# Lending one of four PSUM banks to the weight conversion during the first block

## The chip, the cores and the metric

The kernel runs on one core of one Trainium2 chip. The metric is the time of one execution on that core in microseconds (us), as the median of several runs. A core has five engines that run side by side, each through its own instructions in order: TensorE (PE) multiplies matrices into PSUM, VectorE (DVE), ScalarE (ACT) and GpSimd (POOL) work on elements, and SyncE (SP) issues transfers. PSUM has eight banks; a bank holds 512 numbers of 32 bits in each of 128 partitions. SBUF is the large working memory.

## The reference

The first part is causal attention with a forget gate, for 4 batches, 8 heads, 576 positions and 64 numbers per head; then two layers on the 2304 tokens follow, each 512 to 2048 to 512:

```python
scores = scale * np.matmul(q, k.transpose(0, 1, 3, 2))
cum = np.cumsum(np.maximum(s, 0.0), axis=-1)
bias = -(cum[:, :, :, None] - cum[:, :, None, :])
scores = np.where(causal, -1000000000.0, scores + np.minimum(bias, 0.0))
attn = softmax(scores)                   # max, exp, sum, divide
x = np.matmul(attn, v)                   # tokens x 512

h = x @ w_in;  g = s * relu(h)**2 + b;                      x = g @ w_out
h = x @ w_in2; g = relu(h) + alpha * np.minimum(h, 0.0);    out = g @ w_out2
```

The four weight matrices come as 64-bit floats, which the kernel reads as pairs of 32-bit words.

## The kernel before

*Attention* is cut into 32 units (batch, half of the queries, pair of heads). For each head of a unit, `scores` multiplies q and k into a PSUM bank (`sc`), reduces on DVE with the bias (L461), takes exponentials on ACT (L473), and normalises on POOL (L484). `values` transposes the probabilities on PE into a bank (`pt`, L515), copies them to SBUF (L519) and multiplies with v into `av` (L531), from where `xf` is filled (L546).

*The layers* go by blocks of 256 or 512 tokens and by f, 16 slices of 128 of the 2048 columns. `up` multiplies x and w_in (L783), squares the positive part, and splits the result into a high part gh (ACT) and a rest gl (POOL, L131); `down` multiplies with w_out into the accumulators `acc` (L897). Numbers are multiplied in a short 32-bit format, so everything is split into such a pair first. In layer 2 the blocks of 512 tokens take Strassen's seven products: a pair of f has three PSUM tiles, a, b, c (L854); `up_first` multiplies products 1, 6, 5 into a, b, c and `up_second` adds products 7, 2, 3, 4 (L813). The trace names the tiles p and the right-hand sides xs.

*The weights* of layer 1 are converted while the warm-up and block 0 run: 16 packets of a w_in and a w_out slice. `convert` rescales the high words on ACT (L140), then DVE shifts the result left by 3 in place (L141), and DVE takes the low words shifted right by 29 and ors them in (L142). `load_packet` then splits the result: the high part on ACT (L130), the rest on DVE for w_in and on POOL for w_out (L131). Packets 0 to 3 are traced within attention's warm-up (units 0 to 3), packet f + 4 behind `up(f)` of block 0.

*PSUM:* two banks for `acc`, one for `hp`, one for `av`, and four buffers of the tag `b`, for score tiles, transposes, column sums, the wide block's `hp` and layer 2's tiles.

*The order of work* is not as written: a planner with its own model of time goes through all instructions at build time and writes out a fixed order for each engine, in which the trace's order of the source is a priority. A tile of a tag with several buffers gets one that the planner sees free when the tile is first written; a tile of a tag with one buffer waits until the last user of that buffer is done. Each engine then takes its instructions in that order and waits on semaphores. Attention is drawn along by the loop over n = block * 16 + f (L987), which advances it until a share of the units has been traced (`pace`).

Of the kernel before, what the change touches and what calls it, by code (L numbers as in the profile page):

```python
# [19 lines left out]
def tile_forget_attention__then__two_mlps(  # L20
# [79 lines left out]

    def load_constants():
        nc.sync.dma_start(out=gate_s, in_=act_s.partition_broadcast(P))
        nc.sync.dma_start(out=gate_b, in_=act_b.partition_broadcast(P))
        nc.sync.dma_start(out=nalpha, in_=alpha.rearrange("(f p) -> p f", p=P))
        nc.vector.tensor_scalar(out=nalpha, in0=nalpha, scalar1=-1.0, scalar2=None, op0=ALU.mult)
        nc.vector.tensor_scalar(out=gate_s, in0=gate_s, scalar1=1.0 / W_SCALE, scalar2=None, op0=ALU.mult)
        nc.vector.tensor_scalar(out=gate_b, in0=gate_b, scalar1=1.0 / W_SCALE, scalar2=None, op0=ALU.mult)

    def sum_gates(first):
# [13 lines left out]
        tp = ps.tile([P, 5, B * H], F32, tag="b", bufs=4, name="tp")  # L123
# [10 lines left out]
    def convert(raw, wt):  # L134

        low, high = raw[:, :, 0], raw[:, :, 1]

        nc.scalar.activation(wt.bitcast(F32), high.bitcast(F32), AF.Prelu, scale=REBASE, alpha=-(2.0**32))  # L140
        nc.vector.tensor_scalar(out=wt, in0=wt, scalar1=3, scalar2=None, op0=ALU.logical_shift_left)  # L141
        nc.vector.scalar_tensor_tensor(  # L142
            out=wt, in0=low, scalar=29, in1=wt, op0=ALU.logical_shift_right, op1=ALU.bitwise_or
        )
# [71 lines left out]
    def load_packet(layer, f):  # L216
# [3 lines left out]
        for n, src in enumerate((wi, wo)):  # L220
# [7 lines left out]
            convert(src, wt)  # L228
# [8 lines left out]
    def sum_columns():  # L237
# [5 lines left out]
        total = ps.tile([P, 512], F32, tag="b", name="colsum", bufs=4)  # L243
# [4 lines left out]
        turned = ps.tile([P, 512], F32, tag="b", name="colsum_t", bufs=4)  # L248
# [29 lines left out]
    class Unit:  # L278
# [21 lines left out]
        def bank(self, tag, name):  # L300
# [9 lines left out]
            return ps.tile([P, 512], F32, tag="b", name=name, bufs=4)  # L310
# [449 lines left out]
    def mlp_block(layer, t, x):  # L760
# [11 lines left out]
        def up(f):  # L772
            w = packet(layer, f)
            if layer == 0 and count == 1:
                hp = ps_h.tile([P, 512], F32, tag="hp", name=f"hp{layer}_{t}_{f}")
            else:
                hp = ps.tile([P, 512], F32, tag="b", name=f"hp{layer}_{t}_{f}", bufs=4)
# [68 lines left out]
        def up_first(f):  # L846
# [7 lines left out]
            a, b, c = (ps.tile([P, 512], F32, tag="b", name=f"p{z}_{name}", bufs=4)[:, :T] for z in range(3))  # L854
# [132 lines left out]
    for n in range(len(BLOCKS) * NF):  # L987
# [4 lines left out]
        late.append((down, finish, f, up(f)))  # L992
        if layer == 0 and t == 0 and f + AHEAD < NF:
            with tc.issue_after(relus[f - 1]) if f else nullcontext():
                packet(0, f + AHEAD)
            for g in range(f + AHEAD + 1, min(f + AHEAD + 3, NF)):
                fetch(0, g)
        if n == NF - 2:
# [53 lines left out]
```

## Time and profile before

| what | us |
|---|---|
| median of three runs | 1041.06 |
| lowest, highest run | 1039.58, 1042.63 |
| the profiled execution | 1040.97 |
| its span, first to last instruction | 1039.2 |
| PE busy in it | 1019.4 |
| DVE busy in it | 681.3 |
| ACT busy in it | 672.4 |
| POOL busy in it | 457.6 |

Up to about 61 us PE works on attention's units 0 to 3 and on filler products (L97). Block 0's first product starts at 61.67 us. The profile gives each engine's busy time; an instruction that stands and waits for a port of the memory counts as busy, so its duration is to be compared with the shortest of its kind. PE's matmuls overlap one another; that PE is busy does not mean that it goes at full rate.

### The profile page before, as it was taken

Reading aid. Unit: us, or ns where it says so; the run is one execution under the profiler, and the core shown is the slowest. Engines: PE = TensorE matmul, PEld = TensorE weight load, DVE = VectorE, ACT = ScalarE, POOL = GpSimd, SP = SyncE. Lnnn points to the kernel's source line nnn. Section 1 sums busy time; section 2 is a strip of 40 time slices with the busy share of each in tenths; the row PEclk is TensorE's granted clock in tenths of the full one; section 3 lists DMA queues with packets and bytes.
Section 4 is the critical chain, followed back from the end, with each engine's and each line's share of the span. In section 5 each row is a group of like instructions: output and inputs, shape, how many; then the busy total and the mean of one; then the engine's idle time right before and its main releaser. Section 6 shows DMA issues by size and latency. Waiting matters only on the chain. (4 is left out here: it accounts for less than half of the span.)

```text
span 1039.2 us, 20636 instructions
## 1 busy us (share of the span) xinstructions
PE 1019.4 (98%) x6952; PEld 925.8 (89%) x6952; DVE 681.3 (66%) x1605; ACT 672.4 (65%) x1669; POOL 457.6 (44%) x876
## 2 busy tenths in 40 slices
PE   9899999999999999999999999999999999999997
PEld 4568899999999999999999888888899999999996
DVE  6979865787676776677655865857665456455443
ACT  5877876777787877778776776645454455445433
POOL 5656775666677666777562000574611011001000
PEclk9999999999999999999999999999999999999999
DMA  7988433343232432334215762645644335334331
GB/s 167 255 211 239 132 68 70 71 93 79 40 92 64 102 72 52 79 68 91 66 35 173 240 192 74 207 147 170 196 163 142 103 112 172 103 99 136 104 104 46
DMA packets 197930, 125.45 MB, mean 121 GB/s; under 512 B 138496, under 2 KB 167936, under 8 KB 197824
## 3 DMA queue, kind: packets, MB, share of 16 engines
q1 hardware_dynamic: 193744, 123.56, 42.8%
q8 instruction: 55, 0.90, 0.4%
q10 hardware_dynamic: 4080, 0.57, 0.3%
q14 instruction: 51, 0.42, 0.1%
HBM read 106.19 MB, written 17.90 MB: 119 GB/s over the span
## 5 line engine op out<-in xcount | busy, mean ns | idle before, releaser
L783 PE MATMUL hp<-xh,w 128*128 128x256 f32 (+1 forms) x1024 | 229.0, 300 | 0.3 <-ACT r L802 0.3
L907 PE MATMUL acc<-w,ring 128*128 128x512 f32 x864 | 214.6, 392 | 1.1 <-DVE ring L131 0.7
L907 PEld LDWEIGHTS acc<-w,ring 128*128 128x128 f32 x864 | 155.8, 188 | 29.3 <-DVE ring L131 1.1
L783 PEld LDWEIGHTS hp<-xh,w 128*128 128x128 f32 x1024 | 171.4, 189 | 6.2 <-ACT r L802 0.5
L897 PE MATMUL acc<-gh,w 128*128 128x256 f32 x896 | 172.4, 286 | 0.5 <-ACT res L926 0.5
L783 PE MATMUL hp<-xl,w 128*128 128x256 f32 (+1 forms) x512 | 152.6, 298 | 0.0
L897 PEld LDWEIGHTS acc<-gh,w 128*128 128x128 f32 x896 | 136.0, 189 | 3.2 <-issue 1.6
L883 POOL TENSOR_TENSOR cc<-u,t 128x256 f32<-128x256 f32 x32 | 26.1, 817 | 235.5 <-DVE u L874 201.5
L897 PE MATMUL acc<-gl,w 128*128 128x256 f32 x448 | 118.7, 288 | 2.2 <-POOL gl L131 2.2
L484 POOL TENSOR_SCALAR probs<-probs,sm 64x64 f32<-64x64 f32 (+4 forms) x160 | 91.0, 581 | 60.5 <-DVE sm L481 49.9
L473 ACT ACTIVATE probs<-probs,nm 64x64 f32<-64x64 f32 (+4 forms) x160 | 90.0, 563 | 38.5 <-DVE nm L461 32.7
L131 POOL TENSOR_TENSOR gl<-r,gh 128x256 fp32r<-128x256 f32 x112 | 89.5, 799 | 48.6 <-ACT gh L130 42.1
L817 PE MATMUL p<-xs,sums 128*128 128x256 f32 x768 | 104.7, 282 | 0.4 <-DVE u L859 0.4
L783 PEld LDWEIGHTS hp<-xl,w 128*128 128x128 f32 x512 | 97.1, 190 | 3.3 <-issue 0.4
L817 PEld LDWEIGHTS p<-xs,sums 128*128 128x128 f32 x768 | 98.0, 189 | 2.1 <-DVE u L859 0.6
L461 DVE CUSTOM_DVE_ANT_0 probs<-sc,probs 128x320 f32<-128x320 f32 (+3 forms) x160 | 68.2, 427 | 41.2 <-PE sc L460 32.8
L817 PEld LDWEIGHTS p<-xs,w 128*128 128x128 f32 x576 | 79.0, 189 | 8.7 <-DVE u L874 2.0
L802 ACT ACTIVATE r<-hp 128x256 f32<-128x256 f32 (+1 forms) x144 | 58.0, 403 | 44.1 <-PE hp L783 33.2
L817 PE MATMUL p<-xs,w 128*128 128x256 f32 x576 | 82.3, 282 | 2.4 <-DVE u L874 1.5
L897 PEld LDWEIGHTS acc<-gl,w 128*128 128x128 f32 x448 | 80.1, 188 | 5.0 <-POOL gl L131 2.8
L828 DVE SCALAR_TENSOR_TENSOR ph<-pl,misc,ph 128x512 f32<-128x512 f32 x64 | 51.7, 807 | 42.4 <-ACT pl L844 42.4
L515 PE MATMUL pt<-ident,probs 128*128 128x128 f32 x480 | 74.3, 275 | 4.6 <-POOL probs L484 4.4
(149 smaller groups left out, 2116.8 us busy)
## 6 DMA issues: line engine op xcount, KB each, us to landing
sums<-sums_d SPq DMA_DIRECT2D x128, 256.0 KB, 2.7
wi<-in_moe_w_in_dram SPq DMA_DIRECT2D x32, 512.0 KB, 4.7
wo<-in_moe_w_out_dram SPq DMA_DIRECT2D x32, 512.0 KB, 4.8
cum<-cum_d SPq DMA_DIRECT2D x32, 288.0 KB, 3.7
sums_d<-w SPq DMA_DIRECT2D x64, 128.0 KB, 1.8
cum<-cum_d SPq DMA_DIRECT2D x30, 160.0 KB, 3.0
nat<-in_k_dram SPq DMA_DIRECT2D x64, 72.0 KB, 2.5
x_d<-res SPq DMA_DIRECT2D x18, 256.0 KB, 2.2
```

The lines of the kernel that those rows point to most:

```text
L131: lo_eng.tensor_tensor(out=lo, in0=src, in1=hi.bitcast(F32), op=ALU.subtract)
L461: nc.vector.tensor_tensor_reduce(out=pt[:rows, j0:j1], in0=scr, in1=pt[:rows, j0:j1], scale=SCALE if flip else -SCALE, scalar=init, op0=AL ...
L473: nc.scalar.activation(pt[:rows, :n], pt[:rows, :n], AF.Exp, bias=nm[:rows, m : m + 1], scale=1.0 if flip else -1.0, accum_out=sm[:rows, m ...
L484: nc.gpsimd.tensor_scalar(out=probs[r][:rows, :n], in0=probs[r][:rows, :n], scalar1=sm[:rows, m : m + 1], scalar2=1.0, op0=ALU.mult, op1=A ...
L515: nc.tensor.transpose(tp[:, o : o + P], u.probs[h][r][:, k0 : k0 + P], ident)
L783: nc.tensor.matmul(hs, a[:, c], b[c], start=(n == 0), stop=(n == len(terms) * NCC - 1))
L802: relus.append(nc.scalar.activation(r, hs, AF.Relu, scale=1.0 / W_SCALE).ins)
L817: nc.tensor.matmul(bank, lhs[:, c * P : (c + 1) * P], rhs[:, c], start=(start and c == 0 and z == 0), stop=(c == 1 and z == 2), skip_group ...
L828: nc.vector.scalar_tensor_tensor(out=r, in0=u, scalar=nalpha[:, f : f + 1], in1=r, op0=ALU.mult, op1=ALU.add).ins
L883: nc.gpsimd.tensor_tensor(out=cc[:, T:], in0=u3, in1=t5, op=ALU.add)
L897: nc.tensor.matmul(banks[d] if count == 2 else acc[d // 2][:, d % 2], a[:, d * P : (d + 1) * P], b, start=(f == 0 and (d % 2 == 0 or count ...
L907: nc.tensor.matmul(banks[m], a[:, m * P : (m + 1) * P], b, start=(f == 0 and b is woh and a is gh), stop=(f == NF - 1 and a is gl),)
```

## The change

The shift writes its result into a tile given by the caller, and the shift-and-or reads it from there. While packets 4 to 15 are traced (behind `up` at n = 0 until n = 12), that tile (`bits`) lies in PSUM bank `b3`; otherwise it is the old place. Further, the four buffers of the tag `b` become four tags `b0` to `b3` with one buffer each, and a counter gives each new tile its turn: of four, or of three (`b0` to `b2`) as long as the bank is lent. This holds in the whole program, in layer 2 as well. The lines behind the new function have numbers higher by up to 10.

```diff
+    turn, lent = [0], []
+
+    def bank(name, n=None):
+
+        if n is None:
+            turn[0] += 1
+            n = turn[0] % (3 if lent else 4)
+        return ps.tile([P, 512], F32, tag=f"b{n}", name=name, bufs=1)
+
...
-    def convert(raw, wt):
+    def convert(raw, wt, shifted):
 
         low, high = raw[:, :, 0], raw[:, :, 1]
...
         nc.scalar.activation(wt.bitcast(F32), high.bitcast(F32), AF.Prelu, scale=REBASE, alpha=-(2.0**32))
-        nc.vector.tensor_scalar(out=wt, in0=wt, scalar1=3, scalar2=None, op0=ALU.logical_shift_left)
+        nc.vector.tensor_scalar(out=shifted, in0=wt, scalar1=3, scalar2=None, op0=ALU.logical_shift_left)
         nc.vector.scalar_tensor_tensor(
-            out=wt, in0=low, scalar=29, in1=wt, op0=ALU.logical_shift_right, op1=ALU.bitwise_or
+            out=wt, in0=low, scalar=29, in1=shifted, op0=ALU.logical_shift_right, op1=ALU.bitwise_or
         )
...
-            convert(src, wt)
+            convert(src, wt, bank(f"bits{f}_{n}", 3).bitcast(U32) if lent else wt)
...
-            return ps.tile([P, 512], F32, tag="b", name=name, bufs=4)
+            return bank(name)
...
-                hp = ps.tile([P, 512], F32, tag="b", name=f"hp{layer}_{t}_{f}", bufs=4)
+                hp = bank(f"hp{layer}_{t}_{f}")
...
-            a, b, c = (ps.tile([P, 512], F32, tag="b", name=f"p{z}_{name}", bufs=4)[:, :T] for z in range(3))
+            a, b, c = (bank(f"p{z}_{name}")[:, :T] for z in range(3))
...
         late.append((down, finish, f, up(f)))
+        if n == 0:
+            lent.append(3)
         if layer == 0 and t == 0 and f + AHEAD < NF:
...
+        if n == NF - AHEAD:
+            lent.clear()
```

The other places with the tag `b` (the transposed sums of gates, the two tiles of column sums) go through `bank` in the same way.

The planner's order changes on every engine. First, DVE at the end of the warm-up: `wt0_4_0` and `wt0_4_1` are the two halves of packet 4, `sm_0_3_0_1` the sums of unit 3's second head, `xl0` the rest of x for block 0. Before:

```order
L141 TENSOR_SCALAR wt0_4_0_901<-wt0_4_0_901 128x512
L131 TENSOR_TENSOR xl0_0_870<-xf0_433,xh0_0_869 128x256
L142 SCALAR_TENSOR_TENSOR wt0_4_0_901<-wi0_4_272,wt0_4_0_901 128x512
L375 STREAM_TRANSPOSE turned_0_0_1_695<-nat_0_0_1_564 128x832
L131 TENSOR_TENSOR w0_3_0_11_654<-wt0_3_0_645,w0_3_0_12_653 128x512
L435 TENSOR_SCALAR probs_0_0_1_0_817<-cum0_0_0_1_573,cumT_93 128x448
L435 TENSOR_SCALAR probs_0_0_1_0_817<-cum0_0_0_1_573,cumT_93 128x576
L141 TENSOR_SCALAR wt0_4_1_905<-wt0_4_1_905 128x512
L480 TENSOR_SCALAR sm_0_3_0_1_723<-sm_0_3_0_1_723 128x3
L142 SCALAR_TENSOR_TENSOR wt0_4_1_905<-wo0_4_273,wt0_4_1_905 128x512
L481 RECIPROCAL sm_0_3_0_1_723<-sm_0_3_0_1_723 128x3
```

And now:

```order
L140 TENSOR_TENSOR xl0_0_870<-xf0_433,xh0_0_869 128x256
L486 TENSOR_SCALAR sm_0_3_0_1_723<-sm_0_3_0_1_723 128x3
L441 TENSOR_SCALAR probs_0_0_1_0_817<-cum0_0_0_1_573,cumT_93 128x448
L441 TENSOR_SCALAR probs_0_0_1_0_817<-cum0_0_0_1_573,cumT_93 128x576
L487 RECIPROCAL sm_0_3_0_1_723<-sm_0_3_0_1_723 128x3
L140 TENSOR_TENSOR w0_3_0_11_654<-wt0_3_0_645,w0_3_0_12_653 128x512
L467 ISA probs_0_0_1_0_817,nm_0_0_1_0_815<-sc0_3_0_0_0_1_827,probs_0_0_1_0_817 128x448
L467 ISA nm_0_0_1_0_815 128x1
L467 ISA probs_0_0_1_0_817,nm_0_0_1_0_815<-sc0_4_0_0_0_1_840,probs_0_0_1_0_817 128x320
L467 ISA nm_0_0_1_0_815 128x1
L467 ISA probs_0_0_1_0_817,nm_0_0_1_0_815<-sc0_4_320_0_0_1_843,probs_0_0_1_0_817,nm_0_0_1_0_815 128x256
L467 ISA nm_0_0_1_0_815 128x1
```

Packet 4's first shift (now to `bits4_0`) and all that follows of it have gone behind unit 3's last reciprocal and behind the score reductions of unit 4 (`sc0_3_0_0_0_1` and the next two).

Second, PE at the end of block 0: `av1_0_3_1` is the second head of unit 7, the last that block 1 needs; `acc0_0` block 0's accumulators, where `gh0_0_12` is its f = 12; `hp0_1_0` the first up-product of block 1. Before:

```order
L897 MATMUL acc0_0_1_880<-gh0_0_12_2013,w0_12_2_50_1672 128x256
L897 MATMUL acc0_0_1_880<-gh0_0_12_2013,w0_12_2_49_1673 128x256
L897 MATMUL acc0_0_1_880<-gl0_0_12_2014,w0_12_2_50_1672 128x256
L531 MATMUL av1_0_3_1_1790<-pf_0_3_1_1_0_1796,vn_0_3_1_1475 128x256 x2
L897 MATMUL acc0_0_1_880<-gh0_0_12_2013,w0_12_2_50_1672 128x256
L531 MATMUL av1_0_3_1_1790<-pf_0_3_1_1_1_1811,vn_0_3_1_1475 128x256
L531 MATMUL av1_0_3_1_1790<-pf_0_3_1_1_1_1811,vn_0_3_1_1475 128x192
L531 MATMUL av1_0_3_1_1790<-pf_0_3_1_1_1_1811,vn_0_3_1_1475 128x64
L897 MATMUL acc0_0_1_880<-gh0_0_12_2013,w0_12_2_49_1673 128x256
L897 MATMUL acc0_0_1_880<-gl0_0_12_2014,w0_12_2_50_1672 128x256
L897 MATMUL acc0_0_0_879<-gh0_0_13_2210,w0_13_2_54_1884 128x256
```

And now:

```order
L789 MATMUL hp0_1_0_2367<-xl0_1_1861,w0_0_0_0_204 128x256
L789 MATMUL hp0_1_0_2367<-xh0_1_1860,w0_0_0_63_205 128x256
L903 MATMUL acc0_0_1_880<-gh0_0_14_2266,w0_14_2_57_1959 128x256
L903 MATMUL acc0_0_1_880<-gl0_0_14_2267,w0_14_2_58_1958 128x256
L537 MATMUL av1_0_3_1_1808<-pf_0_3_1_1_0_1814,vn_0_3_1_1485 128x256 x2
L465 MATMUL sc0_2_0_1_0_0_1831<-xs0_1_0_0_1735 128x320
L466 MATMUL sc0_2_0_1_0_0_1831<-xs0_1_0_0_1735,ql00_113 128x320
L537 MATMUL av1_0_3_1_1808<-pf_0_3_1_1_1_1829,vn_0_3_1_1485 128x256
L537 MATMUL av1_0_3_1_1808<-pf_0_3_1_1_1_1829,vn_0_3_1_1485 128x192
L537 MATMUL av1_0_3_1_1808<-pf_0_3_1_1_1_1829,vn_0_3_1_1485 128x64
L465 MATMUL sc1_1_0_1_0_0_2096<-xs1_1_0_0_1736 128x192
L466 MATMUL sc1_1_0_1_0_0_2096<-xs1_1_0_0_1736,ql10_114 128x192
```

The values have moved from the down-products of f = 12, ahead of the last up-product of block 0, to behind the first nine of the twelve products of `hp0_1_0`; the last three come 16 products after the values.

Third, PE in layer 2: `p0`, `p1`, `p2` are a, b and c, with the block and the first f of the pair behind them; the digit in `xs3_4` behind the underscore is the number of the product. Before:

```order
L817 MATMUL p1_3_6_12728<-xs3_4_12121,w1_7_24_9603 128x256 x2
L817 MATMUL p1_3_6_12728<-xs3_4_12121,w1_7_23_9604 128x256
L817 MATMUL p1_3_6_12728<-xs3_4_12121,w1_7_24_9603 128x256 x2
L817 MATMUL p1_3_6_12728<-xs3_4_12121,w1_7_23_9604 128x256
L817 MATMUL p1_3_8_12829<-xs3_6_12116,sums_0_10438 128x256 x6
L817 MATMUL p2_3_8_12830<-xs3_5_12117,sums_0_10438 128x256 x6
```

And now:

```order
L823 MATMUL p0_3_6_12751<-xs3_2_12142,w1_6_20_9577 128x256 x2
L823 MATMUL p0_3_6_12751<-xs3_2_12142,w1_6_19_9578 128x256
L823 MATMUL p0_3_6_12751<-xs3_2_12142,w1_6_20_9577 128x256 x2
L823 MATMUL p0_3_6_12751<-xs3_2_12142,w1_6_19_9578 128x256
L823 MATMUL p0_3_8_12852<-xs3_1_12139,w1_8_28_9695 128x256 x2
L823 MATMUL p0_3_8_12852<-xs3_1_12139,w1_8_27_9696 128x256
L823 MATMUL p2_3_6_12753<-xs3_5_12141,sums_0_10462 128x256 x6
L823 MATMUL p1_3_6_12752<-xs3_7_12143,sums_1_10463 128x256 x6
```

Before, product 5 of pair 8 followed product 4 of pair 6 with product 6 alone between them. Now product 5 of pair 6 stands behind products 2 of its own pair and 1 of the next, well after product 4 of pair 4.

## Rows read from the trace of the kernel before

**Rows 1.** The page's busy time of each engine, share of the span, instructions:

```profile
PE 1019.4 (98%) x6952; PEld 925.8 (89%) x6952; DVE 681.3 (66%) x1605; ACT 672.4 (65%) x1669; POOL 457.6 (44%) x876
```

**Rows 2.** What PE waited for, 0 to 64 us: total, times, longest:

```profile
PE pt L515 <- POOL probs L484: 3.9, 3, 2.8
```

**Rows 3.** Busy us by stage (instructions), then granted clock, DMA share, GB/s:

```profile
20.00:64.00 44.00, 38.83 (x175) 24.02 (x173) 37.45 (x121) 34.51 (x97) 26.22 (x53) 0.92 0.93 246
64.00:126.00 62.00, 60.80 (x391) 50.67 (x391) 57.68 (x114) 51.34 (x123) 39.80 (x54) 1.00 0.73 192
```

**Rows 4.** What PE waited for, 64 to 147 us:

```profile
PE acc L897 <- POOL gl L131: 0.8, 1, 0.8
PE hp L783 <- ACT r L802: 0.3, 1, 0.3
```

**Rows 5.** What PE waited for, 147 us to the end: first and last of nine:

```profile
PE p L817 <- DVE u L874: 1.5, 1, 1.5
...
PE av L531 <- DVE pl L131: 0.2, 1, 0.2
```

**Rows 6.** Groups of DVE instructions, 64 to 126 us: busy us, mean ns, idle before:

```profile
L141 DVE TENSOR_SCALAR wt<-wt 128x512 uint32<-128x512 uint32 x21 | 14.4, 691 | 2.8 <-ACT wt L140 2.6
L142 DVE SCALAR_TENSOR_TENSOR wt<-wi,wt 128x512 uint32<-128x512 uint32 x11 | 11.7, 1060 | 0.2
L142 DVE SCALAR_TENSOR_TENSOR wt<-wo,wt 128x512 uint32<-128x512 uint32 x10 | 8.0, 795 | 0.1
```

**Rows 7.** The shift's line, 64 to 126 us: shortest, median, longest ns:

```profile
L141 DVE TENSOR_SCALAR wt<-wt x21: 404/507/1582, 66.2 to 124.3; 128x512 uint32<-128x512 uint32 x21
```

**Rows 8.** The shift-and-or's line, 64 to 126 us:

```profile
L142 DVE SCALAR_TENSOR_TENSOR wt<-wi,wt x11: 679/1008/1776, 67.6 to 124.7; 128x512 uint32<-128x512 uint32 x11
```

**Rows 9.** DVE in order of time, 109 to 112.5 us: start, us:

```profile
109.28 0.42 DVE L141 TENSOR_SCALAR wt<-wt 128x512 uint32<-128x512 uint32 x1
109.62 1.78 DVE L142 SCALAR_TENSOR_TENSOR wt<-wi,wt 128x512 uint32<-128x512 uint32 x1
```

**Rows 10.** POOL in order of time, 109 to 112.5 us:

```profile
109.50 1.36 POOL L131 TENSOR_TENSOR w<-wt,w 128x512 fp32r<-128x512 f32 x1
110.81 1.17 POOL L131 TENSOR_TENSOR gl<-r,gh 128x256 fp32r<-128x256 f32 x1
```

**Rows 11.** The score reduction's line, 64 to 126 us:

```profile
L461 DVE CUSTOM_DVE_ANT_0 probs<-sc,probs x11: 477/608/624, 67.1 to 122.3; 128x448 f32<-128x448 f32 x6, 128x320 f32<-128x320 f32 x5
```

**Rows 12.** The copies out of PSUM, 64 to 126 us, on DVE:

```profile
L519 DVE COPY pf<-pt x6: 649/679/681, 64.9 to 120.4; 128x512 f32<-128x512 f32 x6
```

**Rows 13.** The page's costliest groups: a shape with two SBUF tensors:

```profile
L828 DVE SCALAR_TENSOR_TENSOR ph<-pl,misc,ph 128x512 f32<-128x512 f32 x64 | 51.7, 807 | 42.4 <-ACT pl L844 42.4
```

**Rows 14.** Groups of POOL instructions, 64 to 126 us:

```profile
L131 POOL TENSOR_TENSOR gl<-r,gh 128x256 fp32r<-128x256 f32 x10 | 9.2, 916 | 1.0 <-ACT gh L130 0.7 <-POOL w L131 0.3
```

**Rows 15.** DVE in order of time, 50.9 to 53 us:

```profile
52.36 0.16 DVE L481 RECIPROCAL sm<-sm 128x3 f32<-128x3 f32 x1
```

**Rows 16.** POOL in order of time, 40 to 66 us:

```profile
52.69 1.52 POOL L484 TENSOR_SCALAR probs<-probs,sm 64x64 f32<-64x64 f32 x3
```

**Rows 17.** PE in order of time, 50 to 64.5 us:

```profile
53.76 0.55 PE L515 MATMUL pt<-ident,probs 128*128 128x128 f32 x3 [2.79 <-POOL probs L484]
```

**Rows 18.** The chain that ended last: start, us, what:

```profile
762.58 2.86 PE p L817 x24
765.43 2.74 PE acc L907 x12
```

**Rows 19.** Groups of ScalarE instructions, 64 to 147 us:

```profile
L546 ACT COPY xf<-av 64x192 f32<-64x192 f32 x8 | 2.5, 310 | 0.1
...
L130 ACT CAST xh<-xf 128x256 fp32r<-128x256 f32 x4 | 1.5, 404 | 0.0
```

**Rows 20.** The split's second part of x, 120 to 150 us:

```profile
L131 POOL TENSOR_TENSOR xl<-xf,xh x2: 724/955/1186, 128.2 to 145.8; 128x256 fp32r<-128x256 f32 x2
```

**Rows 21.** DVE in order of time, 763 to 778 us:

```profile
774.90 0.42 DVE L884 TENSOR_TENSOR cc<-p,t 128x256 f32<-128x256 f32 x1 [0.20 <-PE p L817]
```

More of the change, by code (lines that the diff above doesn't have):

```diff
@@ L122, in sum_gates @@
             first.cums.append(rows)
-        tp = ps.tile([P, 5, B * H], F32, tag="b", bufs=4, name="tp")
+        tp = bank("tp")[:, : 5 * B * H].rearrange("p (r h) -> p r h", h=B * H)
         for r, (i0, i1) in enumerate(IB):
@@ L242, in sum_columns @@
         nc.scalar.copy(ones_r, ones)
-        total = ps.tile([P, 512], F32, tag="b", name="colsum", bufs=4)
+        total = bank("colsum")
         for n in range(2 * NF):
@@ L247, in sum_columns @@
         nc.scalar.copy(colw, total)
-        turned = ps.tile([P, 512], F32, tag="b", name="colsum_t", bufs=4)
+        turned = bank("colsum_t")
         for d in range(NCC):
```

## The prediction

> **What bounds the kernel now.** I read the busy times first, then the stages, then what TensorE waited for in each stage, and last the operations that the change touches. TensorE (PE) is busy for 98% of the span [rows 1], so a change can give back only time in which PE waits or runs at its lower clock, and can cost only by making new time of that kind. The reader should look for that time. Up to 64 us, the warm-up, PE's listed wait for normalised probabilities is 3.9 us in three waits, the longest 2.8 [rows 2], and the mean granted clock from 20 to 64 us is 0.92 [rows 3], so part of this stretch ran at the lower of the two levels (1.2 and 2.4 GHz). From 64 to 147 us, the first block with its edges, PE lists 0.8 us behind a POOL subtraction and 0.3 us behind ScalarE [rows 4]: 1.1 us. In the remaining 890 us there are nine groups of waits, from 1.5 us down to 0.2 [rows 5]. So the first block is bound by PE, yet VectorE (DVE) is close behind: 57.68 of 62 us [rows 3].
>
> In the first block, DVE's largest work is the conversion of weights: 21 shifts of 691 ns, and 21 shift-and-ors of 1060 ns (from wi) and 795 ns (from wo) in the window [rows 6]. These means hide two populations: the same shift takes 404 ns at its shortest and 1582 at its longest [rows 7], the same shift-and-or 679 and 1776 [rows 8]. The row at 109.62 us shows what stretches one: its 1.78 us are the rest of the POOL subtraction that it met (begun at 109.50 and 1.36 long, so 1.24 us of rest) and something near its ordinary time [rows 9, 10]. DVE operations that read PSUM do not stretch: the score reduction, with one operand in PSUM and one in SBUF, stays between 477 and 624 ns over eleven instances of two widths [rows 11], the 512-wide copy out of PSUM between 649 and 681 [rows 12], with POOL busy 39.80 of the same 62 us [rows 3].
>
> **The change part by part.** *The shift.* It now writes PSUM. No row shows DVE writing PSUM. Bounds: 404 ns from below, the unstretched shift [rows 7]; 807 ns from above, the mean of a 512-wide operation with two SBUF tensors [rows 13]. I take 670, near the 512-wide copy that has one side in PSUM. 21 shifts then take 21 x (691 - 670) = 0.4 us less: the stretch goes, and so does the fast form. *The shift-and-or.* It now has one operand in PSUM and one in SBUF, which is the form of the score reduction. I take 680 ns, its unstretched time: 11 x (1060 - 680) + 10 x (795 - 680) = 5.3 us less. Together DVE is relieved of 5.8 us out of 57.68; with both edits at 404 and 680 it would be 21 x 0.287 + 5.3 = 11.4, with both at 807 it would be -21 x 0.116 + 11 x 0.253 - 10 x 0.012 = 0.2.
>
> The row shows a stretched shift-and-or with two SBUF tensors while POOL ran [rows 9, 10]. The Trainium skill (SBUF — State Buffer, Who interferes with whom) says that a DVE instruction with two SBUF inputs, or in a two-port mode, contends with GpSimd, and that one with at most one SBUF input outside those modes does not; by that rule the trace agrees, in [rows 11], and without it the 5.3 us of the shift-and-ors would stay on DVE and the sum would be rival E's. Against the change speaks the Trainium skill (VectorE: DVE Perf Modes, What auto-detection actually checks): the two-port mode of a one-source operation wants source and destination in SBUF, so the shift loses it; 512 elements at one per cycle of 0.96 GHz would be an estimated 533 ns plus overhead, beside 404 at present. By that rule alone DVE would have 21 x 0.27 = 5.6 us more from the shifts if none were stretched now; the sum by it would lose the block's gain and end at 1040.5. The measured mean of 691 says that most are stretched.
>
> What of DVE's relief reaches the end? PE's waits in this block end on POOL's subtraction gl and on ScalarE, both fed through these queues: 1.1 us. POOL's gl takes 916 ns there [rows 14] and also loses its opponent. I count 1.0 us of the 1.1 as gained; the rest of the relief lands in idle time of DVE.
>
> *The order at the start.* Before, both shifts and both shift-and-ors of packet 4 stand ahead of the reciprocal for unit 3's second head, as the first piece of order shows; now packet 4 comes behind it. The reciprocal ended at 52.36 + 0.16 us [rows 15], POOL's normalisation ran from 52.69 [rows 16], and PE's longest wait ended there [rows 17]. What now stands behind is 2 x (0.404 + 0.679) = 2.2 us at unstretched times. But the first block's up-projection cannot finish its first f before the fourth piece of x is split, and up to that subtraction DVE has the same work in both orders, except one 832-wide transpose more and two small operations on sums less. So I count 0.8 us of this wait as gained, between 0 and 3.9.
>
> *One bank fewer.* Three banks serve the scores and transposes of units 4 to 7 while bits hold the fourth. The wait for the lent bank itself costs nothing on DVE: shift and shift-and-or are both on DVE, in order, so only the first shift waits, for attention's last tile there. Behind that shift stand the other DVE operations of attention, and PE's scores wait for those. PE's cover is the block's own products, placed between them. At the block's end the last head's values move from among the down-products of f = 12 to behind block 1's first nine products (second piece of order); from there to the piece that needs them stand twelve down-products at 2.86 / 24 = 0.119 us [rows 18] and four score products, 1.4 us and some. The path beside them is a copy of 0.31, a cast of 0.404 [rows 19], and a POOL subtraction of 0.724 to 1.186 [rows 20] for the second product: 1.4 to 1.9 us. I count 0.3 us lost; from 0 to 3.
>
> *Fixed banks for the rest.* Before, a tile took whichever of the four buffers was free in the planner's account; now its bank is its turn. In layer 2 a pair's third product needs the bank of the previous pair's second. The third piece of order shows it: that product used to follow six others (0.7 us), now twelve 256-wide products (1.43 us) and a down-projection of twelve 512-wide ones of 2.74 us [rows 18] stand between it and the last product in its bank, 4.2 us. The reader of the bank takes 0.42 us [rows 21]. Cover is ample: 0, unless DVE is over 3 us late. Attention in blocks 1 to 6 also gets another order; its few waits, no group over the 1.5 us of [rows 5], may grow or shrink. I count 0.
>
> Sum: -1.0 - 0.8 + 0.3 = -1.5 us. The profiled execution took 1040.97 us around its span of 1039.2, 0.1 under the median of 1041.06; 1040.97 - 1.5 = 1039.5.
>
> **The rivals.** *B, the relief pays in full.* The first block's 1.1 us and the warm-up's 3.9 us of waits all go: 1041.0 - 5.0 = 1036.0; below that, if time at the lower clock goes as well (0.08 of 44 us, 3.5 us of work), 1032.5. For it: the warm-up's longest wait is the one whose releaser moves forward, and DVE has 37.45 of 44 us to do there. Against: the same DVE work up to the fourth split.
>
> *C, the short bank is the bound: slower.* With three banks, attention's next score has to wait until DVE has read one two tiles earlier, so PE issues it late, the last head's values come late, and block 1's first product stands still. The place is the edge of blocks 0 and 1; the price is a wait of the warm-up's kind, 2.8 us each [rows 2], once inside the block and once at its edge: 1041.0 + 5.6 - 1.0 = 1045.6. It decides from the point where values arrive more than the 1.4 us of cover behind. For it: the second piece of order, in which attention stands later. Against: DVE, which all of it passes through, is relieved.
>
> *D, layer 2 waits for its turn.* 32 pairs by 0.42 us is 13.4, so 1053. Against: the cover of 4 us.
>
> *E, the change doesn't relieve DVE.* Writing PSUM takes 807 ns and the shift-and-ors still stretch: 21 x 0.116 = 2.4 us more on DVE, 60.1 of 62, all of it on the path: 1043.4.
>
> **How the numbers follow.** This kernel's measurement tells about 0.3%, 3.1 us, from no change: faster is under 1037.9, slower over 1044.2. My forecast has 0.53, B 0.27, C 0.13, D 0.02, E 0.05. Faster is B: 0.27. Same is the forecast and half of E, 0.55; slower C, D and the other half, 0.18. The range goes from 1034.5, within B, to 1044.5, short of C's full price, as the new order of the whole program has no row that bounds it; the forecast's own range, from its terms, is 1041.0 - 5.0 to 1041.0 + 3.0.
>
> **What would show it.** Shifts near 670 ns with hardly any spread and no shift-and-or over 0.75 us confirm the relief; shifts at 800 or stretched ones refute it. DVE's busy time from 64 us to the end of the first block should fall by about 5 us. PE's wait for normalised probabilities near 51 us should be shorter, but the first up-projection should begin near 61 us still. A PE wait of over 1.5 us at the edge of blocks 0 and 1, ended by attention's split, would be C; idle gaps on PE before the third product of a layer-2 pair, D. I am wrong if the first block's products end several us earlier or later with none of these.

## The result: 14.7 us slower, not 1.5 faster

The changed kernel takes 1055.66 us (median of four runs, 1055.54 to 1056.82) where the kernel before takes 1040.91 beside it: a ratio of 1.0142, with a 95% interval from 1.0127 to 1.0158. The profiled execution took 1055.54 us around a span of 1053.4. The forecast was 1039.5, its range ended at 1044.5. So it was wrong, although what the change does to VectorE came out as foretold.

The page's busy times after, which answer to [rows 1]:

```profile
PE 1026.2 (97%) x6952; PEld 927.8 (88%) x6952; DVE 673.9 (64%) x1605; ACT 669.0 (64%) x1669; POOL 448.0 (43%) x876
```

TensorE has the same 6952 products. It is busy for 6.8 us longer and idle for 7.4 us longer (27.2 of the span against 19.8). The relief stands in the rows of the two lines, after, from 60 to 150 us (shortest/median/longest ns); they answer to [rows 6 to 8]:

```profile
L147 DVE TENSOR_SCALAR bits<-wt x21: 678/689/695, 66.5 to 121.9; 128x512 uint32<-128x512 uint32 x21
L148 DVE SCALAR_TENSOR_TENSOR wt<-wi,bits x11: 673/683/687, 67.5 to 122.6; 128x512 uint32<-128x512 uint32 x11
L148 DVE SCALAR_TENSOR_TENSOR wt<-wo,bits x10: 674/686/689, 69.6 to 121.1; 128x512 uint32<-128x512 uint32 x10
```

No shift and no shift-and-or is stretched any more. The stages, after, as in [rows 3]:

```profile
20.00:64.00 44.00, 39.11 (x180) 24.53 (x178) 38.34 (x122) 34.15 (x97) 26.03 (x52) 0.92 0.93 245
64.00:126.00 62.00, 61.38 (x398) 50.79 (x398) 50.50 (x111) 49.74 (x119) 37.17 (x53) 1.00 0.71 190
...
147.00:200.00 53.00, 49.57 (x359) 46.46 (x358) 31.23 (x109) 34.38 (x104) 32.83 (x82) 0.97 0.30 65
```

From 64 to 126 us DVE, the third busy time of a row, falls from 57.68 to 50.50, by 7.2 us. What PE waits for up to 64 us, after (total, times, longest), which answers to [rows 2]:

```profile
PE sc L463 <- DVE turned L381: 2.8, 1, 2.8
PE pt L521 <- POOL probs L490: 1.8, 2, 1.6
```

The wait for normalised probabilities shrank by 2.1 us, and a wait for a DVE transpose of 2.8 took its place. From 64 to 150 us, after, for [rows 4]:

```profile
PE av L537 <- DMA vn<-in_v_dram: 0.6, 1, 0.6
PE acc L903 <- POOL w L140: 0.4, 1, 0.4
```

Again 1.0 us in place of 1.1. So the first block's waits did not shrink. The loss comes behind it. From 150 to 660 us, blocks 1 to 7, after (the first five groups), where [rows 5] had nothing over 1.5 in the whole rest:

```profile
PE av L537 <- DVE pl L140: 3.5, 3, 1.5
PE pt L521 <- POOL probs L490: 1.5, 3, 1.0
PE av L537 <- POOL probs L445: 1.1, 1, 1.1
PE sc L465 <- DVE sm L487: 1.0, 1, 1.0
PE av L537 <- ACT r L808: 0.9, 1, 0.9
```

In all five the product that waits is one of attention's. The longest wait of the first group, on PE in order of time, after:

```profile
153.57 0.28 PE L789 MATMUL hp<-xh,w 128*128 128x256 f32 x1
153.80 0.50 PE L537 MATMUL av<-ph,vs_all 128*128 128x320 f32 x2
155.78 0.50 PE L537 MATMUL av<-pl,vs_all 128*128 128x320 f32 x2 [1.48 <-DVE pl L140]
```

And DVE in the same stretch:

```profile
152.90 1.42 DVE L441 TENSOR_SCALAR probs<-cum,cumT 64x64 f32<-64x64 f32 x3
154.25 0.25 DVE L486 TENSOR_SCALAR sm<-sm 128x3 f32<-128x3 f32 x1
154.32 0.83 DVE L381 STREAM_TRANSPOSE turned<-nat 128x640 f32<-128x640 f32 x1
155.08 0.78 DVE L140 TENSOR_TENSOR pl<-pt,ph 128x512 fp32r<-128x512 f32 x2
```

And on ACT, the cast `ph` that `pl` needs, and the read of the up-projection's bank:

```profile
152.99 0.67 ACT L139 CAST ph<-pt 128x512 fp32r<-128x512 f32 x2
...
155.87 0.38 ACT L808 ACTIVATE r<-hp 128x256 f32<-128x256 f32 x1 [1.90 <-POOL gl L140]
```

The split `pl`, for which PE stands still, has its input from 153.66 us on (152.99 and 0.67), but it stands in DVE's queue behind the bias of another head (L441) and a transpose (L381). DVE is not short of time there, with 31.23 of 53 us busy from 147 to 200 us (last row of the stages). It is the order in which the work stands. The next up-projection, which PE's queue holds behind the product that needs `pl`, could not have filled the gap: the bank of `hp` is read only from 155.87 to 156.25, and that read waited 1.90 us for POOL's gl. The wait also has an aftermath: the clock granted from 147 to 200 us is 0.97 (same row), and in the kernel before it is 1.00:

```profile
147.00:200.00 53.00, 53.00 (x417) 51.57 (x417) 32.30 (x110) 36.55 (x108) 32.64 (x88) 1.00 0.31 68
```

By these two rows about 1.6 us (0.03 of 53) of the loss there is time at the lower level.

To place the whole loss I use one figure for all kernels, the **delay**: for every product on PE the time from its start to the next start, less what the same pair of kinds usually takes in the kernel before (the value that a fifth of such pairs stay under). The rest, the time at usual spacing, is 965 to 969 us in every kernel of the table, so the delay is where they differ. Pairs that are rare have no firm usual value; counted in other ways, differences between kernels in a cell move by up to about 2 us. In us, by stretch of the trace:

```
kernel                          0-62  62-220  220-300  300-700  700-end    sum
before                          17.2    15.9      6.0     16.9      6.8   62.7
after                           17.0    25.4      8.0     20.3      9.5   80.1
fixed turn alone                17.0    25.2      3.6     17.4      9.3   72.4
fixed turn, one jump by 1       18.1    23.1      7.0     20.5      9.2   77.8
fixed turn, one jump by 2       17.7    23.4      3.6     18.8      8.7   72.0
after, lent n = 9 to 12 only    18.3    23.0      4.4     18.4      8.3   72.4
free choice, lent n = 0 to 2    17.3    28.2      6.3     17.8      6.9   76.5
free choice, lent n = 10 to 12  16.3    19.0      6.0     17.0      6.3   64.6
```

After loses 9.5 us up to 220 us (blocks 0 and 1), 2.0 up to 300, 3.4 up to 700 and 2.7 behind it, 0.2 less at the start, and its usual spacing takes 2.7 less (966.5 for 969.2): 14.7 between the first and the last product, 14.2 by the spans.

The stretches hold the same time and not the same work, so I also compare kernels at equal work. Where the kernel before is at 220, 300 and 500 us, after is 8.9, 9.8 and 13.7 us later with the same sum of product widths left, and the kernel with the fixed turn alone (first experiment) 8.2, 5.9 and 6.7. So up to 220 us the loan adds next to nothing to the turn, and the two part behind it. From layer 2's first product to PE's last, 2130 products, before takes 343.7 us, after 345.2 and the turn alone 345.1: layer 2 costs 1.5 us, and not the 2.7 of the table's last column.

### The profile page after: what moved, and what is told of

Read it like the earlier page. It is cut to its first block, busy times and chain, and to the rows that moved or that the text cites. A ratio compares the mean times of both kernels' runs of the same rounds, so it can differ in the third digit from the quotient of the medians.

```text
span 1053.4 us, 20734 instructions
## 1 busy us (share of the span) xinstructions
PE 1026.2 (97%) x6952; PEld 927.8 (88%) x6952; DVE 673.9 (64%) x1605; ACT 669.0 (64%) x1669; POOL 448.0 (43%) x876
## 5 line engine op out<-in xcount | busy, mean ns | idle before, releaser
L140 POOL TENSOR_TENSOR gl<-r,gh 128x256 fp32r<-128x256 f32 x112 | 85.1, 760 | 66.5 <-ACT gh L139 41.7
L490 POOL TENSOR_SCALAR probs<-probs,sm 64x64 f32<-64x64 f32 (+4 forms) x160 | 93.7, 598 | 43.9 <-DVE sm L487 30.6
L823 PE MATMUL p<-xs,sums 128*128 128x256 f32 x768 | 108.0, 282 | 0.4 <-DVE u L865 0.4
L823 PEld LDWEIGHTS p<-xs,sums 128*128 128x128 f32 x768 | 100.3, 189 | 2.9 <-DVE u L865 0.6
L823 PE MATMUL p<-xs,w 128*128 128x256 f32 x576 | 84.7, 282 | 2.2 <-DVE u L880 1.5
L521 PE MATMUL pt<-ident,probs 128*128 128x128 f32 x480 | 76.8, 277 | 3.3 <-POOL probs L490 3.3
L884 DVE TENSOR_TENSOR u<-p,u 128x256 f32<-128x256 f32 x32 | 13.5, 423 | 90.0 <-PE p L823 90.0
```

Source lines behind the costliest of these rows:

```text
L140: lo_eng.tensor_tensor(out=lo, in0=src, in1=hi.bitcast(F32), op=ALU.subtract)
L490: nc.gpsimd.tensor_scalar(out=probs[r][:rows, :n], in0=probs[r][:rows, :n], scalar1=sm[:rows, m : m + 1], scalar2=1.0, op0=ALU.mult, op1=A ...
L521: nc.tensor.transpose(tp[:, o : o + P], u.probs[h][r][:, k0 : k0 + P], ident)
L823: nc.tensor.matmul(bank, lhs[:, c * P : (c + 1) * P], rhs[:, c], start=(start and c == 0 and z == 0), stop=(c == 1 and z == 2), skip_group ...
L884: nc.vector.tensor_tensor(out=u2, in0=c, in1=u2, op=ALU.add)
```

## Experiments

Sixteen kernels in four groups, each beside runs of the kernel before (medians from 1040.2 to 1041.0). T1: the fixed turn of the banks costs. T2: one bank fewer puts attention behind. T3: the shift that writes PSUM disturbs TensorE.

**The turn alone.** `lent.append(3)` and `lent.clear()` are left out, so nothing is lent and four banks take turns.

> Only the fixed turn of four banks is kept; no bank is lent and the shift stays in place in SBUF. Theory T1 (the fixed turn of banks, over the whole program, makes the planner's order for attention worse, so that TensorE waits in blocks 1 to 6): 1052 to 1057 us, with the shifts stretched as before (mean near 690 ns) and waits scattered from 140 to 560 us. Rival T2 (three banks instead of four in block 0 put attention behind, and it has to be caught up): 1039 to 1043, since four banks stay. Rival T3 (the shift that writes PSUM disturbs others): 1039 to 1043.

Measured: 1048.12 us, ratio 1.0075 (1.0052 to 1.0098). The turn alone costs 7.2 us, half of the loss: less than T1's 1052 to 1057, and more than T2 and T3 allow.

**The loan with free choice.**

```diff
-        return ps.tile([P, 512], F32, tag=f"b{n}", name=name, bufs=1)
+        return ps.tile([P, 512], F32, tag="b", name=name, bufs=4)
```

> The shift writes PSUM during block 0, but its tile and all the others take whichever of four buffers the planner finds free; no fixed turn. T1: 1037 to 1040, the relief of block 0 (up to 2.7 us less lost time up to 140 us) without the loss behind it. T2: 1044 to 1052, since the bits still take a bank from attention for most of block 0. T3: 1053 to 1057.

Measured: 1054.45 us, ratio 1.0132 (1.0104 to 1.0160). The loan without the turn costs 13.5, so the parts don't add: 7.2 + 13.5 is far over 14.7. T1 is off by 14 us, T2's range by 2.5; T3's holds it, and the next run tests T3.

**The bank withheld, the shift in place.** In after, `convert(src, wt, wt)`: the fourth bank lies idle from n = 0 to 12.

> The fixed turn, with the fourth bank withheld from attention during block 0 as in the changed kernel, but the shift stays in place in SBUF, so that nobody uses that bank. T1: 1055 to 1060, the changed kernel's loss without its relief. T2: 1055 to 1060 as well. T3: 1039 to 1043.

Measured: 1055.30 us, ratio 1.0143 (1.0120 to 1.0166), as after. T3 falls. The shift-and-ors stretch again, and DVE is at 58.63 us from 64 to 126:

```profile
64.00:126.00 62.00, 61.00 (x394) 50.69 (x394) 58.63 (x110) 49.37 (x117) 40.65 (x53) 1.00 0.67 188
```

The line of its shift-and-ors from wi:

```profile
L148 DVE SCALAR_TENSOR_TENSOR wt<-wi,wt x11: 676/772/1774, 67.9 to 123.5; 128x512 uint32<-128x512 uint32 x11
```

So 8.1 us more on DVE make no difference to the end: in this form the relief is worth nothing that can be measured.

**A bank of its own for the bits,** three by free choice for the rest, in the whole program:

```diff
-        return ps.tile([P, 512], F32, tag=f"b{n}", name=name, bufs=1)
+        if n is not None:
+            return ps.tile([P, 512], F32, tag="bits", name=name, bufs=1)
+        return ps.tile([P, 512], F32, tag="b", name=name, bufs=3)
```

> Free choice among three banks for attention and layer 2 in the whole program, and a bank of its own for the bits of block 0 that nobody uses afterwards. T1: 1038 to 1042: one bank fewer everywhere, yet no fixed turn. T2: 1052 or more, as the shortage now lasts for the whole program. T3: 1053 to 1057.

Measured: 1074.57 us, ratio 1.0326 (1.0299 to 1.0353). Three banks for good are too few, as T2 had it (1052 or more): PE waits 10.3 us in ten waits for probabilities.

**How long the loan lasts.** Four kernels with `n == 5`, `n == 2`, `n == 15` for the return, and one with `n == 9` for the loan; a fifth withholds the bank, with the shift in place, until n = 28, and a sixth in block 3.

> The change with the bank given back at n = 5 in place of n = 12: only the bits of packets 4 to 8 lie in PSUM, packets 9 to 15 are shifted in place, and attention has its fourth bank back for the second half of block 0. T2 (the shortage puts attention behind, and the price grows with its length): between the turn alone (1048.1) and the whole change (1055.7), near 1051, and TensorE's waits at the edge of blocks 0 and 1 shorter than in the changed kernel. T4 (the price is paid once, at the switch between three and four banks, whenever it comes): 1055, as the whole change, with the waits moved to the place of the switch. T5 (any new order costs so much, the shortage has no part): no ordered relation, anything from 1045 to 1057.

> The change with the bank given back at n = 2 in place of n = 12: only the bits of packets 4 to 6 lie in PSUM. T2 (price by the length of the shortage): 1.2 us over the turn alone, 1049.3. U (the shortage only tips the planner's order of the blocks that follow, and that order is what costs): its PE order of blocks 1 and 2 is a new one, neither that of the change nor of the turn alone, so its time is free, 1046 to 1056; but from block 3 on its order is that of the kernel with the bank lent from n = 9, instruction for instruction, so from 310 us on both must lose the same to within 1 us.

> The change with the bank given back at n = 15, three steps later: attention has three banks for the whole of block 0. T2: 7.5 x 15 / 12 = 9.4 over the turn alone, 1057.5, and no less than the change's 1055.7. U: its PE order is that of the change in block 0 (726 of 728 instructions) but another one from block 1, and from block 6 that of the turn alone; it may come out below the change, 1048 to 1055, although the bank is away for longer.

> The change with the bank lent from n = 9 to n = 12 only: bits of packets 13 to 15 in PSUM. T2: 1.8 us over the turn alone, 1050. U: free, 1046 to 1056, but from 310 us on the same loss as with the bank lent from n = 0 to 2, to within 1 us, since the PE order is the same there.

> Fixed turns, the shift in place, and the fourth bank withheld from n = 0 to n = 28, through block 0 and most of block 1, more than twice as long as in the change. T2: more than the 1055.3 of withholding in block 0 alone; with the same price per step, 7.2 x 28 / 12 = 16.8 over the turn alone, 1065. T4 (the price is paid at the switch): 1055.

> Fixed turns as in the change, the shift in place throughout, and the fourth bank withheld (used by nobody) from n = 48 to n = 60, in block 3, and not in block 0. T2: the wide block's up-projections take their tiles from the same banks there, so attention has even less left: at least the 7.2 us that withholding cost in block 0, so 1055 to 1060, with the waits in block 3 and behind it. T6 (block 0 alone is sensitive, since DVE is busy there for 57.7 of 62 us and cannot catch up): block 3, where DVE has idle time, bears three banks: 1048 to 1050, as the turn alone.

Measured:

```
bank away for            us        ratio (95% interval)
0 steps (turn alone)     1048.12   1.0075 (1.0052 to 1.0098)
2 (n = 0 to 2)           1048.47   1.0075 (1.0056 to 1.0094)
3 (n = 9 to 12)          1045.65   1.0049 (1.0034 to 1.0064)
5 (n = 0 to 5)           1055.07   1.0136 (1.0111 to 1.0160)
12 (after)               1055.66   1.0142 (1.0127 to 1.0158)
15 (n = 0 to 15)         1056.44   1.0152 (1.0135 to 1.0170)
28 (through block 1)     1063.49   1.0231 (1.0214 to 1.0247)
12 (in block 3)          1051.93   1.0115 (1.0099 to 1.0130)
```

(The return at n = 5 comes behind packet 9, so six packets' bits lie in PSUM there and not the five that the expectation names; the return at n = 2 behind packet 6.) This isn't a price per step: 2 or 3 steps cost nothing over the turn alone, 5 cost as much as 15. T2's price per step doesn't fit within block 0. T4 had 5 steps right, but 2 and 3 steps have the same switch and pay nothing. T5's range holds every row but the 28 steps, since it was so wide; that any new order costs so much is refuted by 2 and 3 steps.

What 5 and 12 steps share, and the kernel with the bank withheld too, is the order that the planner writes for PE from block 2 to the end: it is the same in all three, instruction for instruction, and it is another one than that of the turn alone. The same holds for time: from block 3's first up-product to PE's last product these three take 743.7, 743.5 and 743.3 us. The kernels with 2 and with 3 steps share theirs from block 3 on; they take 741.3 and 740.0 from there, 1.3 apart where I had allowed 1. So a new theory, U: the loan tips the planner into another order of the blocks behind it, and that order costs. (U was set up after the first eight kernels; the expectations from the 2 steps on name it.) The 15 steps came out at 1056.4, above the 1048 to 1055 that U had left open, and 1.1 under T2's 1057.5; this run leans to T2.

Two more kernels keep T2 alive for longer loans or later ones. With the bank away through block 1, the first of the twelve products of block 2's first up-projection starts at 217.7 us and the last only at 242.0, and PE waits in between for attention (215 to 245 us, first two groups, and the stage's row):

```profile
PE pt L521 <- POOL probs L490: 3.2, 2, 3.0
PE sc L465 <- DVE nm L467: 1.9, 4, 1.0
```

```profile
215.00:245.00 30.00, 21.90 (x113) 18.12 (x112) 24.78 (x63) 20.19 (x47) 16.73 (x31) 0.72 0.43 96
```

PE is busy for 21.90 of 30 us, at a mean granted clock of 0.72, so part of this stretch ran at the lower level and lost 8.4 us of work (0.28 of 30). In all this kernel takes 15.4 us more than the turn alone.

In block 3 twelve steps cost 3.8 over the turn alone, half of block 0's price; neither the 7.2 of T2 nor the nothing of T6.

**The relief without a bank.** In the kernel before, `if f < AHEAD` ahead of the shift.

> The kernel before (any free bank of four) with the shift of packets 4 to 15 left out: that part of the conversion isn't computed, nothing stands in its place, and no bank is lent. DVE loses 21 shifts of 691 ns in the first block, 14.5 us, about twice of what the change relieves it of. If DVE's load in block 0 is what TensorE waits for: 1036 or less. By my reading of the profile (PE waits 1.1 us there): 1039 to 1041, no difference that can be told.

Measured: 1038.28 us, ratio 0.9976 (0.9961 to 0.9990). DVE's stage in that kernel:

```profile
64.00:126.00 62.00, 61.60 (x400) 51.53 (x399) 42.17 (x102) 52.38 (x126) 44.13 (x59) 1.00 0.75 206
```

15.5 us less on DVE give 2.5 by the ratio, and 1.0 to 4.1 by its interval. The change relieves DVE of half as much.

**Five buffers by free choice,** the bank of `hp` among them (`bufs=5` at each tile of `b`, and the tag `b` for those of `hp`).

> The kernel before with free choice of five buffers: the bank of hp joins the four, and hp of the narrow blocks, the transposes that had it, and the fourth accumulator of the wide blocks take theirs from the five. No bank is lent, nothing is left out. If the number of banks that attention can draw on is what sets the waits in blocks 1 to 6 (T2 taken to its other end): 1030 to 1036. If four are enough and only the order counts (U): 1040 to 1050, as another order of the whole program.

Measured: 1105.08 us, ratio 1.0620 (1.0580 to 1.0661), the worst of all. Both theories had it wrong. More choice isn't more room. I read it so that `hp`, without a bank of its own, now competes with attention, but no run here tests that. Over the span PE's first wait is

```profile
PE pt L515 <- POOL probs L484: 31.3, 27, 3.5
```

**The order without the loan.** In the turn alone, a line ahead of the packets of block 0: `if n == 6: turn[0] += 1`, and in a second kernel `+= 2`.

> Fixed turns of four, nothing lent, the shift in place; at n = 6 the counter jumps once by one, so one bank is passed over. Four banks serve throughout: there is no shortage. From block 3 on its PE order is the change's, instruction for instruction. U (the order of the blocks behind is what the loan costs): the change's loss without any loan, 1053 to 1056. T2 (the shortage costs): 1048, as the turn alone.

> As the kernel whose counter jumps by one, but it jumps by two. From block 2 on its PE order is that of the turn alone. U: 1048, within 1.5 us. T2: 1048 too. The rival that any jump costs (the jump itself makes a wait in block 0): 1053 to 1056, as with one.

Measured: 1052.85 us, ratio 1.0122 (1.0105 to 1.0138), and 1046.96, ratio 1.0069 (1.0054 to 1.0084). The jump by one comes out just under U's 1053 to 1056 and well over T2's 1048; the jump by two is where U had it. With the jump by one the order is the change's from block 4 on, and nearly so in block 3; the expectation had said block 3. A jump by one costs 5.9 us more than a jump by two; nothing is lent in either, four banks serve throughout. The difference between the two in delay lies mostly where after's over the turn alone does (220 to 300 us: 3.4; 300 to 700 us: 1.7). What PE waits for from 300 to 660 us, after:

```profile
PE av L537 <- DVE pl L140: 1.0, 1, 1.0
PE acc L903 <- POOL gl L140: 0.7, 1, 0.7
PE av L537 <- DVE xf L555: 0.5, 1, 0.5
```

The same with a jump by one:

```profile
PE av L537 <- DVE pl L140: 1.0, 1, 1.0
PE acc L903 <- POOL gl L140: 0.7, 1, 0.7
PE av L537 <- DVE xf L555: 0.6, 1, 0.6
```

And with a jump by two, the whole list:

```profile
PE hp L789 <- ACT r L808: 0.6, 1, 0.6
PE pt L521 <- POOL probs L490: 0.4, 1, 0.4
```

The waits come with the order, not with the loan. The sharpest comparison is from block 4's first up-product to PE's last product, where six kernels with turns have the same 4425 products left:

```
order from block 4 on   kernel                     us
the change's            after                      677.8
                        bank withheld              677.6
                        lent n = 0 to 5            677.9
                        jump by 1, nothing lent    677.7
the turn alone's        turn alone                 673.4
                        jump by 2, nothing lent    673.7
```

So about 4.2 us go with the order alone, whether a bank is lent or not. That is U, shown for these kernels. It covers 4.4 of the 7.5 us that the loan costs over the turn; the other 3 arise before block 4, and no kernel without a loan shows them.

**The loan with free choice, short.** In the loan with free choice, the return at `n == 2`, or the loan at `n == 10`.

> Free choice of four buffers as before, bits of packets 4 to 6 in one of the four (given back at n = 2), the others shifted in place. From block 2 on its PE order is that of the kernel before, in block 1 nearly (561 of 567 instructions). U: the time of the kernel before, 1040 to 1043, where the same with all twelve packets took 1054.5. T2: 2/12 of that loss, 1043.3, which these rounds can hardly tell from it; both are refuted by 1046 or more.

> Free choice of four buffers, bits of packets 14 and 15 in one of them (lent from n = 10 to n = 12). From block 2 on its PE order is that of the kernel before. U: 1040 to 1043. The rival that the place counts (the loan lies at the end of block 0, where the wait for the last head's values decides): 1046 or more, with TensorE's waits at the edge of blocks 0 and 1.

Measured: 1051.82 us, ratio 1.0113 (1.0098 to 1.0128), and 1043.25, ratio 1.0014 (0.9992 to 1.0036). Both have the PE order of before from block 2 on, and lose nothing there: from block 2's first up-product to PE's last product the three take 813.5 us (before), 813.5 and 813.1. So the first refutes U for free choice, and T2 as well: three packets, a quarter of the loan, cost 10.9, all of it up to 220 us. DVE, the third busy time of a row, from 62 to 100 us in the kernel before, in that one, and in the one with the loan at the end:

```profile
62.00:100.00 38.00, 37.92 (x242) 31.29 (x241) 33.95 (x72) 31.73 (x77) 23.42 (x33) 1.00 0.84 224
```

```profile
62.00:100.00 38.00, 37.38 (x233) 30.28 (x231) 22.06 (x62) 25.21 (x60) 14.82 (x29) 1.00 0.66 158
```

```profile
62.00:100.00 38.00, 37.82 (x236) 30.82 (x236) 35.00 (x72) 31.77 (x75) 23.76 (x33) 1.00 0.89 233
```

With the loan at the start DVE does 12 us less in that stretch, because it stands. What it waits for there:

```profile
DVE probs L464 <- PE sc L460: 11.0, 4, 4.4
DVE wt L144 <- ACT wt L143: 3.9, 2, 2.2
```

The longest of these, DVE in order of time:

```profile
66.94 0.17 DVE L484 RECIPROCAL sm<-sm 128x2 f32<-128x2 f32 x1
71.51 0.49 DVE L464 CUSTOM_DVE_ANT_0 probs<-sc,probs 128x320 f32<-128x320 f32 x1 [4.40 <-PE sc L460]
```

And PE:

```profile
69.27 0.28 PE L900 MATMUL acc<-gl,w 128*128 128x256 f32 x1
...
70.67 1.24 PE L460 MATMUL sc<-turned 64*128 64x320 f32 x4
```

PE issues that score only at 70.67, behind a whole down-projection and nine products of the next up-projection, and the conversions of weights stand behind its reduction on DVE. So 12 us of DVE's work comes later, and from 100 to 151 us PE waits in its turn (its longest wait, then the columns of the stages):

```profile
PE pt L518 <- POOL probs L487: 4.0, 1, 4.0
```

```profile
100.00:151.00 51.00, 41.95 (x268) 36.83 (x269) 43.02 (x84) 36.94 (x88) 36.90 (x47) 0.93 0.56 153
```

PE is busy for 41.95 of 51 us there. The whole loan with free choice shows the same wait of DVE, 9.6 us. The loan at the end, two packets, can't be told from before, so the rival that the end of block 0 is the dear place falls. That the late score is the planner's choice and not forced by the lent bank, no run tests.

## Why the prediction was wrong

*What bounds the kernel.* Right: PE does, and a change can cost only by new waits. It did.

*The shift and the shift-and-or.* Right in mechanism and size: 689 and 683 ns (means) for my 670 and 680. DVE lost 7.2 us for my 5.8: 5.3 by the two edits, the rest because it also has less else to do in the window. By the Trainium skill (SBUF — State Buffer, Who interferes with whom) a DVE instruction with at most one SBUF input, outside the two-port modes, does not contend with GpSimd. The trace agrees: 673 to 689 ns with POOL busy for 37.17 of 62 us, and up to 1774 in place.

*What of the relief reaches the end: 1.0 us.* Nothing measurable in after: the two waits went, two others of 1.0 us came. That little of it reaches the end was right, as 15.5 us off DVE give 2.5.

*The order at the start: 0.8.* The wait moved to the transpose behind: 3.9 us became 1.8, with 2.8 new. The delay up to 62 us is 17.0 for 17.2. I had named that transpose as one more thing on the path, and still counted a gain.

*One bank fewer: 0.3, up to 3.* The place, the edge of blocks 0 and 1, was right for one wait of 1.48 us and two smaller ones behind it. Three banks for 2 or 3 steps cost nothing over the turn. But the whole loan costs 7.5 over the turn, and 4.4 of it go with another order from block 4 on, which a kernel without any loan pays as well. The term looked at the wait that the missing bank makes, not at what the planner does with it.

*Fixed banks for the rest: "I count 0."* This is the step that failed. The turn alone costs 7.2 us. In layer 2 the cover of 4.2 us held for the third product, and rival D's 13.4 did not come, yet it isn't free: from its first product to PE's last one every kernel with turns takes 344.4 to 345.4 us, those with free choice of four 342.7 to 343.7. The larger part is attention in blocks 0 and 1 (9.3 us of delay for the turn alone, 8.2 at equal work, of which it gives back over 2 in block 2). I had seen that the order of all blocks is new, and had no row that bounds it; I took 0 and let the range end where my known terms did. The range should have been open above.

*Rival C* had the right sign, and 1045.6 for a price: it counted a wait inside block 0 and one at its edge, where the delay comes from block 1 on and is spread over many. *B*, the relief in full, is refuted by the shift left out: 2.5 us, 4.1 at most by the interval, for twice the relief.

*The signs.* The shifts without spread, the shorter wait for probabilities and the first up-projection at 61.1 us came as I had said. The wait at the edge of blocks 0 and 1 was 1.48 us, just under the 1.5 that I had set for C. None of my signs concerned the order of the blocks behind, where the loss is.

What stays open: why the planner's order with fixed turns costs 8 to 9 us in blocks 0 and 1, and which of its choices at the return of the bank leads to the dear order. About half of the former can be named. From 62 to 160 us PE waits in the turn alone for

```profile
PE pt L521 <- POOL probs L490: 1.9, 2, 1.7
PE av L537 <- POOL vs_all L140: 0.9, 1, 0.9
PE av L537 <- DVE pl L140: 0.6, 1, 0.6
PE acc L903 <- ACT gh L139: 0.5, 1, 0.5
```

3.9 us in all, where the kernel before has the two waits of [rows 4], 1.1 us; and behind these waits the clock granted from 140 to 160 us is 0.91 for 1.00, another 1.8 us. Of the 14.2 us by which after's span grew, PE's idle time holds 7.4; the rest lies in its busy time, in part at the lower clock, and otherwise in products that start a little late with no releaser shown. No version that does the whole work beat the kernel before.

## What to carry to other kernels

Where a planner writes the order, a change of buffers is a change of the whole program's order, and its price must be bounded from other orders of the same kernel, not from the waits at the place of the edit: here kernels with the same products and the same turns, and a bank away for 0 to 15 steps, lay between 1045.7 and 1056.4 us. Before lending a resource, ask what the relief is worth with nothing taken for it; leaving the operation out told that at once (2.5 us). And a buffer's count is no measure of room: five by free choice, with `hp` among them, were 64 us worse than four and one set apart.

## What the runs showed of the hardware

A 512-wide 32-bit shift on DVE that writes PSUM takes 678 to 695 ns over 21 instances (after), against 404 to 1582 in place in SBUF (before): neither the short times nor the stretched ones occur, and the means are nearly the same, 689 and 691. Where PE waited long, its clock fell: the granted clock is 0.93 from 100 to 151 us in the kernel with three packets lent by free choice, where PE is busy for 41.95 of 51 us, so about 3.6 us (0.07 of 51) of its 10.9 are time at the lower level.
